# Where and when the raw words of w_val and w_out are loaded, and when w_val's are converted

## The chip, the cores and the metric

The kernel runs on one core of a Trainium2 chip. The metric is the device time in microseconds (us) of one execution. Five engines work beside each other, each through its own list of instructions in order: PE (TensorE, matrix multiplications), ACT (ScalarE), DVE (VectorE), POOL (GpSimd), and SP (SyncE), which here issues every transfer (DMA). An instruction waits at the head of its engine's list until what it needs is there, and everything behind it waits too.

## The reference

Three stages are applied to four batches of 576 positions and 512 features (8 heads of 64), all float32 at the interface.

- Attention: a low-resolution attention over positions averaged by four, repeated four times, plus a local attention in which position i sees positions i-3 to i+3.
- A Fourier mixing and an MLP: `u = x + real(fft over positions and features)`, `un` = `u` normalized over features, then `u + relu(un @ w_ch1) @ w_ch2` (512 to 2048 to 512).
- A gated projection: `gate = sigmoid(5-tap causal convolution over positions)`, output `(gate * (x @ w_val)) @ w_out` (both 512 x 512).

The weights come in as 64-bit floats; the kernel gets them as pairs of 32-bit words, low word and high word, and has to make float32 of them itself.

## The kernel before, in words

The MLP is cut into 12 units of 192 positions, three per batch. A unit's first product (`ph`, line 1047, in groups of 24 matmuls) and second product (`pc`, line 1065) are each made of three 16-bit products, because every float32 operand is split into a 16-bit high part and a 16-bit rest (`hh` and `hl`, `uh` and `ul`, `yh` and `yl`; of weights `hi` and `lo`). Each group of `pc` therefore needs `hh`, which ACT writes (line 1051), and `hl`, which DVE writes (line 165, called from `h_group`). The first unit alone is computed in float32 (`steps32`, lines 1009 and 1022), while the weights are still being split.

The weights pass through four steps: a transfer brings raw words, 1024 words of 64 bits per row and position for w_ch1 and w_ch2, 2 x 512 for w_val and w_out; three DVE instructions make float32 of a raw tile (`to_f32`: a TENSOR_SCALAR at line 283, then two SCALAR_TENSOR_TENSORs at line 165); a norm of the whole matrix gives a power of two; and `conv_w` writes `hi` (ACT, line 344) and `lo` (DVE, line 165). There are 20 positions: 0 to 7 hold w_ch1, 8 to 15 w_ch2, 16 and 17 w_val, 18 and 19 w_out. Their storage is W0 and a ring of ten double tiles; the tile named W17 in the lists below holds `W[17]` and `W[18]`, the one named W19 holds `W[19]` and `W[20]`. `hi` and `lo` of position i go into the storage `W[i]`, while the float32 values of that position sit in `W[i+1]`. So the split of one position must be finished by DVE before ACT can start the next: the 16 splits of w_ch1 and w_ch2 are one chain that goes back and forth between ACT and DVE.

While the first unit runs, batch 1's attention runs beside it. Its local attention goes in three groups: band and scores on PE (`dS`), maximum on DVE (`dmx`), exponentials on ACT (line 536), normalization on DVE (`dP`, line 168), transposes on PE (`dPT`), a copy on ACT (`PT`, line 563), products with v on PE (`dO`), copies into X on ACT (line 583). The squares of v for the pooled v are ACT's at line 425; its sums are POOL's. After each unit the five convolution taps of the gated stage follow: products on ACT (`tap`, line 1123), sums on POOL (line 171).

In the kernel before, the raw words of w_val and w_out land in the two tiles of the tag "k" and "v" in the pool `qkv`, which hold batch 1's windows of v until the local attention's last products have read them. `word_w` issues each load and its conversion together, half a position at a time, so eight loads and 24 DVE instructions. The order of the program is made by a list of events, each with a place in units of the MLP: `spread` lays a list of steps evenly over a stretch. The table's entry `S_W3 = (1.02, 1.6)` lays all steps of `weights3_steps` over the second unit. A scheduler then sets each engine's list from this order, from priorities (`urgent`) and from its own estimate of time.

Of the kernel before, what the change touches and what calls it, by code (L numbers as in the profile page):

```python
# [12 lines left out]
I32 = mybir.dt.int32  # L13
# [4 lines left out]
B, H, S, D = 4, 8, 576, 64  # L18
# [31 lines left out]
S_S0 = (-11.1, -10.1)  # L50
# [3 lines left out]
S_END = -8.95  # L54
S_F0 = (-8.9, -8.1)
# [1 line left out]
S_N0 = -7.5  # L57
S_W2 = (-7.4, -6.9)
S_C2 = (0.89, 0.94)
S_W3 = (1.02, 1.6)  # L60
N_WARM = (8, 5, 14, 2, 2, 2)
S_G1 = (-6.8, -6.7)
S_G2 = (0.2, 0.44)
# [12 lines left out]
P_TAP = (-0.05, 0.35)  # L76
# [51 lines left out]
def attn_moe_kernel(ctx, tc, q_t, k_t, v_t, w1, w2, w_val, conv_t, w_out, c_feat, c_seq, c_band, c_eye, out):  # L128
    nc = tc.nc
    P = 128  # L130
    w1, w2, w_val, conv_t, w_out = (x.bitcast(I32) for x in (w1, w2, w_val, conv_t, w_out))

    def pool(name, bufs=1, **kw):
        return ctx.enter_context(tc.tile_pool(name=name, bufs=bufs, **kw))
# [29 lines left out]
    def stt(eng, out, in0, scalar, in1, op0, op1):  # L164
        return eng.scalar_tensor_tensor(out=out, in0=in0, scalar=scalar, in1=in1, op0=op0, op1=op1)  # L165
# [16 lines left out]
    def load(**kw):  # L182

        if chain["on"] and chain["last"] is not None:
            with tc.issue_after(chain["last"]):
                i = nc.sync.dma_start(**kw)
        else:
            i = nc.sync.dma_start(**kw)
        chain["last"] = i.ins
# [63 lines left out]
    NPOS = 20  # L253
    ring = [wp.tile([P, 2048], F32, name=f"W{2 * i + 1}") for i in range(NPOS // 2)]
    W = [wp.tile([P, 1024], F32, name="W0")]
# [11 lines left out]
    def rows(dst, src, c, c0, n):  # L267
        load(out=dst, in_=src[c * 128:(c + 1) * 128, 2 * c0:2 * (c0 + n)])
# [3 lines left out]
    def behind(gate, f):  # L272

        if gate is None:
            f()
        else:
            with tc.issue_after(gate):
                f()

    def to_f32(dst, raw, gate=lambda: None):  # L280

        r = raw.rearrange("p (n t) -> p n t", t=2)
        behind(gate(), lambda: V.tensor_scalar(out=dst, in0=r[:, :, 1], scalar1=3, scalar2=0x3FFFFFF8,  # L283
                                               op0=ALU.logical_shift_left, op1=ALU.bitwise_and))
        behind(gate(), lambda: stt(V, dst, r[:, :, 1], -0x40000000, dst, ALU.bitwise_and, ALU.bitwise_or))
        behind(gate(), lambda: stt(V, dst, r[:, :, 0], 29, dst, ALU.logical_shift_right, ALU.bitwise_or))
# [18 lines left out]
    def word_w(i):  # L305
        if i < 16:
            raw = raws.pop(i)
            n = 1024 // len(raw)
            for z, x in enumerate(raw):
                to_f32(W[i + 1].bitcast(I32)[:, z * n:(z + 1) * n], x,  # L310
                       lambda g=(gates, gates2)[i // 8]: g.pop(0) if len(g) > 1 else g[0])
            return
        assert "scored" in st[1]
        for a in range(2):
            raw = qkv.tile([P, 1024], I32, tag="kv"[a], name="raw")
            rows(raw, w_val if i < 18 else w_out, (i % 2) * 2 + a, 0, 512)
            to_f32(W[i + 1].bitcast(I32)[:, a * 512:(a + 1) * 512], raw)

    gram = {}

    def sumsq_w(i, key, first, last):

        if first:
            gram[key] = pst("cv", [P, P]) if key == "wo" else ps_c.tile([P, P], F32, tag="c1", name="gram")
        x = W[i + 1].bitcast(BF16).rearrange("p (n t) -> p n t", t=2)
        for c in range(8):
            blk = x[:, c * 128:(c + 1) * 128, 1]
            behind(st[0]["st2"].ins if i < 8 else None, lambda: T.matmul(
                out=gram[key], lhsT=blk, rhs=blk, start=(first and c == 0), stop=(last and c == 7)))
# [11 lines left out]
    def conv_w(i, s, eng):  # L341

        h_, l_, r_ = hi(i), lo(i), W[i + 1]
        A.activation(out=h_, in_=r_, func=AF.Copy, scale=s[:, 0:1])
        if eng is G:
            A.activation(out=r_, in_=r_, func=AF.Copy, scale=s[:, 0:1])
            G.tensor_tensor(out=l_, in0=r_, in1=h_, op=ALU.subtract)
        else:
            stt(eng, l_, r_, s[:, 0:1], h_, ALU.mult, ALU.subtract)
# [17 lines left out]
    def wv_scale():  # L367
        ps = pst("cv", [P, 512])
        for a in range(4):
            j = pr_t("sqv", [P, 512])  # L370
            A.activation(out=j, in_=W[17 + a // 2][:, (a % 2) * 512:(a % 2) * 512 + 512], func=AF.Square)
            T.matmul(out=ps, lhsT=ones, rhs=j, start=(a == 0), stop=(a == 3))
        mx = keep.tile([P, 1], F32, name="cvmx")
        V.tensor_reduce(out=mx, in_=ps, axis=AX.X, op=ALU.max)
        mx2 = keep.tile([P, 1], F32, name="cvmx2")
        V.tensor_scalar(out=mx2, in0=mx, scalar1=float(DM), scalar2=None, op0=ALU.mult)
        sc["sv"], sc["ivv"] = pow2(mx2, 14, "wv")

    def wo_scale():
        f = trace_w("wo")  # L380
        sc["so"], sc["ivo"] = pow2(f, 14, "wo")
        ivvo = keep.tile([P, 1], F32, name="ivvo")
        mul(V, ivvo, sc["ivv"], sc["ivo"])
        sc["ivvo"] = ivvo
# [3 lines left out]
    st = {}  # L388
# [524 lines left out]
    un = {}  # L913
    mainp = {}

    def main_pools():
        for n, bufs in (("un", 2), ("hg", 3), ("g", 1), ("L", 2), ("tap", 3), ("S", 3)):
            mainp[n] = pool("m_" + n, bufs)

    def l_t(name, shape):  # L920
# [289 lines left out]
    def w_in2(i):  # L1210
        if i >= 11:
            load_w(i)
        word_w(i)

    def w_in(i):
        word_w(i)
# [4 lines left out]
    def weights3_steps():  # L1221
        def first():
            to_f32(cw.rearrange("p a b -> p (a b)").bitcast(I32), craw)

        def a2():
            wv_scale()
            for i in range(16, 18):
                conv_w(i, sc["sv"], G if i in LO_G else V)

        def a3():  # L1230
            for i in range(18, NPOS):
                sumsq_w(i, "wo", i == 18, i == NPOS - 1)
            wo_scale()
            for i in range(18, NPOS):
                conv_w(i, sc["so"], G if i in LO_G else V)
        return [first] + [lambda i=i: word_w(i) for i in range(16, NPOS)] + [a2, a3]

    units = [(b, j) for b in range(B) for j in range(UPB)]
    events = []
# [1 line left out]
    def put(pos, f):  # L1241
        events.append((pos, len(events), f))

    def spread(steps, p0, p1):
        tot = sum(c for c, _ in steps)
        acc = 0.0
        for c, f in steps:
            put(p0 + (p1 - p0) * acc / tot, f)
            acc += c
# [16 lines left out]
    def close():  # L1266
        start.close()
        main_pools()

    assert S_LD[1] <= S_T0[0] and S_L1 <= S_W1[0] and S_T0[1] <= S_S0[0] and S_S0[1] <= S_F0[0] and S_F0[1] <= S_N0  # L1270
    assert S_W1[1] <= S_W2[0] and 8 / 17 < S_C1[0] and S_C1[1] <= S_C2[0] and 15 / 17 < S_C2[0]
    assert S_S0[1] <= S_END <= S_F0[0] and S_C2[1] <= min(S_W3[0], 1 + P_TAP[0])
    put(S_END, close)
    for b in range(1, B):
        steps = attn_steps(b)
# [7 lines left out]
        spread(steps[n1:], *P_E[b])  # L1283
        put(P_L[b], lambda b=b: urgent(lambda: ln(b, 0), "N"))
    w3 = weights3_steps()
    spread([(1.0, f) for f in w3], *S_W3)
    for n, (b, j) in enumerate(units):
        main = mlp_steps(b, j)
        spread([(1.0, f) for f in main], n, n + 1)
# [63 lines left out]
```

## Time and profile before

| | us |
|---|---|
| median of 3 runs | 771.54 (769.82 to 771.86) |
| the profiled execution, its own time | 768.35 |
| its span in the trace | 766.5 |
| PE busy | 695.8 |
| DVE busy | 450.3 |
| ACT busy | 378.1 |
| POOL busy | 183.8 |

Times in the trace count from the start of the span. The first 110 us go to batch 0's attention and Fourier stage, the first unit runs from about 109 to 178 us with batch 1's local attention, and units of 16-bit products follow. Matmuls are pipelined, so a busy share of PE near 100% does not say that it runs at its peak; an idle PE from 110 us on lengthens the kernel unless it makes the time up later.

### The profile page before, as it was taken

Reading aid. Unit: us, or ns where it says so; the run is one execution under the profiler, and the core shown is the slowest. Engines: PE = TensorE matmul, PEld = TensorE weight load, DVE = VectorE, ACT = ScalarE, POOL = GpSimd, SP = SyncE. Lnnn points to the kernel's source line nnn. Section 1 sums busy time; section 2 is a strip of 40 time slices with the busy share of each in tenths; the row PEclk is TensorE's granted clock in tenths of the full one; section 3 lists DMA queues with packets and bytes.
Section 4 is the critical chain, followed back from the end, with each engine's and each line's share of the span. In section 5 each row is a group of like instructions: output and inputs, shape, how many; then the busy total and the mean of one; then the engine's idle time right before and its main releaser. Section 6 shows DMA issues by size and latency. Waiting matters only on the chain.

```text
span 766.5 us, 18498 instructions
## 1 busy us (share of the span) xinstructions
PE 695.8 (91%) x7811; PEld 605.4 (79%) x7811; DVE 450.3 (59%) x897; ACT 378.1 (49%) x1170; POOL 183.8 (24%) x187
## 2 busy tenths in 40 slices
PE   6869579986699998999979999898999999999996
PEld 3535459985688987987869899788799998999893
DVE  3894789769885766256786631656742472532134
ACT  1465211778544636677552766864522435251512
POOL 0400000015421522361231243601410323030300
PEclk8565579999799999999999999999899999999999
DMA  9965347033321110222121001001100000000001
GB/s 227 370 226 166 112 185 208 24 101 117 102 74 56 55 64 16 54 93 77 39 69 64 16 23 34 22 2 54 55 15 2 16 1 30 2 15 2 29 1 42
DMA packets 29004, 54.79 MB, mean 71 GB/s; under 512 B 2133, under 2 KB 17109, under 8 KB 27898
## 3 DMA queue, kind: packets, MB, share of 16 engines
q1 hardware_dynamic: 28922, 53.61, 21.6%
q8 instruction: 61, 1.00, 0.5%
q14 instruction: 21, 0.17, 0.1%
HBM read 46.52 MB, written 9.45 MB: 73 GB/s over the span
## 4 chain that ended last, share of the span: by engine, by line
PE 61%; DVE 20%; ACT 8%; DMA 7%; issue 1%; SPq 1%; POOL 0%; ACTq 0%; DVEq 0%; POOLq 0%
PE pc L1065 19%; PE ph L1047 18%; DVE W L165 6%; PE val L1144 5%; PE out L1160 5%; ACT dP L536 3%; PE po L716 2%; DMA v<-in_v_dram 2%; DVE W L283 2%; DVE fF L787 1%; ACT tap L1123 1%; PE dO L577 1%; PE sc L668 1%; DMA raw<-in_moe_w_out_dram 1%; PE ab L810 1%
## 5 line engine op out<-in xcount | busy, mean ns | idle before, releaser
L1065 PE MATMUL pc<-hh,W 128*128 128x192 f16 x1408 | 199.4, 248 | 3.8 <-ACT hh L1051 3.8
L1065 PEld LDWEIGHTS <-W 128*128 128x128 f16 x2112 | 178.0, 99 | 25.6 <-issue 21.8
L1047 PE MATMUL ph<-uh,W 128*128 128x192 f16 x1408 | 196.4, 247 | 0.1
L1065 PE MATMUL pc<-hl,W 128*128 128x192 f16 x704 | 173.3, 249 | 12.7 <-DVE hl L165 12.7
L1047 PEld LDWEIGHTS <-W 128*128 128x128 f16 x2112 | 176.4, 98 | 7.1 <-issue 5.1
L1047 PE MATMUL ph<-ul,W 128*128 128x192 f16 x704 | 173.7, 247 | 0.0
L171 POOL TENSOR_TENSOR W<-W,tap 128x768 f32<-128x768 f32 x40 | 74.9, 1873 | 141.2 <-ACT tap L1123 109.8
L165 DVE SCALAR_TENSOR_TENSOR hl<-ph,hh 128x384 f16<-128x384 f32 x88 | 48.0, 551 | 98.4 <-ACT hh L1051 98.2
L1051 ACT ACTIVATE hh<-ph 128x384 f16<-128x384 f32 x88 | 42.3, 485 | 72.0 <-PE ph L1047 71.6
L1123 ACT ACTIVATE tap<-X,cw 128x192 f32<-128x192 f32 x180 | 66.5, 446 | 5.5 <-DMA out_dram<-osb 4.7
L1144 PE MATMUL val<-yy,W 128*128 128x192 f16 x576 | 53.3, 246 | 4.0 <-ACT yy L1099 2.3
L1144 PEld LDWEIGHTS <-W 128*128 128x128 f16 x576 | 48.0, 98 | 5.1 <-issue 3.9
L536 ACT ACTIVATE dP<-dS,dmx 128x64 f32<-128x64 f32 x160 | 47.7, 332 | 0.3
L1160 PE MATMUL out<-W,gh 128*128 128x512 f16 x144 | 45.9, 379 | 0.0
L536 ACT ACTIVATION_READ_ACCUMULATOR dP<-dS,dmx 128x1 f32 x160 | 36.2, 226 | 0.0
L1160 PE MATMUL out<-W,gl 128*128 128x512 f16 x72 | 27.3, 379 | 2.1 <-DVE gl L165 2.1
L165 DVE SCALAR_TENSOR_TENSOR W<-W,W 128x1024 int32<-128x1024 int32 x24 | 28.7, 1215 | 0.1
L171 POOL TENSOR_TENSOR vr<-v 72x256 f32<-72x256 f32 x12 | 11.3, 944 | 66.9 <-DMA v<-in_v_dram 64.2
L165 DVE SCALAR_TENSOR_TENSOR yy<-X,s_y,yy 128x768 f16<-128x768 f32 x12 | 19.2, 1601 | 13.5 <-ACT yy L1099 13.4
L682 ACT ACTIVATE E<-sc,nm 72x144 f32<-72x144 f32 x64 | 23.5, 372 | 4.8 <-PE po L716 4.7
L716 PE MATMUL po<-ET,vr 72*64 72x144 f32 x128 | 21.6, 345 | 4.6 <-ACT ET L711 4.6
L1009 PE MATMUL ph<-u,W 128*128 128x192 f32 x128 | 24.8, 350 | 1.0 <-DVE u L945 1.0
(222 smaller groups left out, 1212.4 us busy)
## 6 DMA issues: line engine op xcount, KB each, us to landing
W<-in_moe_w_ch_dram SPq DMA_DIRECT2D x12, 1024.0 KB
v<-in_v_dram SPq DMA_DIRECT2D x32, 144.0 KB
out_dram<-osb SPq DMA_DIRECT2D x18, 256.0 KB
vw<-in_v_dram SPq DMA_DIRECT2D x16, 256.0 KB
X<-in_q_dram SPq DMA_DIRECT2D x6, 576.0 KB
kT<-in_k_dram SPq DMA_DIRECT2D x4, 582.0 KB
dx<-X SPq DMA_DIRECT2D x4, 576.0 KB
dr<-dx SPq DMA_DIRECT2D x4, 576.0 KB
```

The costliest lines, as they stand in the source:

```text
L165: return eng.scalar_tensor_tensor(out=out, in0=in0, scalar=scalar, in1=in1, op0=op0, op1=op1)
L171: return eng.tensor_tensor(out=out, in0=a, in1=b, op=ALU.add)
L536: A.activation(out=s_[:, z, a], in_=pss[par][:, z, a], func=AF.Exp, scale=SCALE, bias=mx[:, par, z, a:a + 1], accum_out=su[:, par, z, a:a ...
L682: A.activation(out=E[:, qc], in_=ps[:, qc], func=AF.Exp, scale=SCALE / 16, bias=nm[:, qc:qc + 1], accum_out=su[:, qc:qc + 1],)
L716: T.matmul(out=po[par * 64:par * 64 + 64], lhsT=d["vr"][:, kc, (a % 2) * 4 + (a // 2) * 2 + par], rhs=ets[par][:, kc], start=(kc == 0), st ...
L1009: i = T.matmul(out=ps[:, e], lhsT=W[kc * 2 + m // 8 + 1][:, o:o + 128], rhs=u()[:, kc, :], start=(kc == 0), stop=(kc == 3))
L1047: T.matmul(out=ps[:, e], lhsT=w1_ap(pw, kc, 2 * g + e), rhs=uh[px][:, kc, :], start=(t == 0), stop=(t == 11))
L1051: A.activation(out=h_, in_=ps, func=AF.Relu)
L1065: T.matmul(out=ps[m // 2][:, m % 2], lhsT=w2_ap(pw, kk, m), rhs=x[px][:, e, :], start=(kk == 0 and (pw, px) == (0, 0) and m % 2 == 0), sto ...
L1123: A.activation(out=g[:, c], in_=X[:, c, c0:c0 + UT], func=AF.Copy, scale=cw[:, c, t:t + 1])
L1144: T.matmul(out=ps[:, e], lhsT=wv_ap(pw, kc, 2 * mh + e), rhs=m_["y"][px][:, kc, :], start=(t == 0), stop=(t == 11))
L1160: T.matmul(out=ps, lhsT=(gh, gl)[px][:, kc, t * 128:(t + 1) * 128], rhs=wo_ap(pw, kc), start=(n == 0), stop=(n == 11))
```

## The change

The step that loads is cut off from the step that converts. `load_w3(i, a)` picks where half a of position i lands: halves (16, 0) and (17, 1) in `W[19]`, halves (16, 1) and (18, 0) in `W[20]`, both free since w_ch2's last raw words were converted; halves (17, 0) and (18, 1) in a new tile `rx`; only the two halves of position 19 still in the tiles "k" and "v". The steps come in two lists with places of their own: w_val's loads and conversions lie over 0.44 to 0.8, within the first unit, and w_out's, with the norms and splits of both, over 1.0 to 1.5.

```diff
-S_W3 = (1.02, 1.6)
+S_W3 = ((0.44, 0.8), (1.0, 1.5))
...
-        assert "scored" in st[1]
         for a in range(2):
+            to_f32(W[i + 1].bitcast(I32)[:, a * 512:(a + 1) * 512], raw3.pop((i, a)))
+
+    raw3 = {}
+
+    def load_w3(i, a):
+
+        if (i, a) in ((16, 0), (17, 1)):
+            raw = W[19].bitcast(I32)
+        elif (i, a) in ((16, 1), (18, 0)):
+            raw = W[20].bitcast(I32)
+        elif i < 19:
+            raw = mainp["rx"].tile([P, 1024], I32, tag="rx", name="raw")
+        else:
+            assert "scored" in st[1]
             raw = qkv.tile([P, 1024], I32, tag="kv"[a], name="raw")
-            rows(raw, w_val if i < 18 else w_out, (i % 2) * 2 + a, 0, 512)
-            to_f32(W[i + 1].bitcast(I32)[:, a * 512:(a + 1) * 512], raw)
+        raw3[i, a] = raw
+        rows(raw, w_val if i < 18 else w_out, (i % 2) * 2 + a, 0, 512)
...
-        for n, bufs in (("un", 2), ("hg", 3), ("g", 1), ("L", 2), ("tap", 3), ("S", 3)):
+        for n, bufs in (("un", 2), ("hg", 3), ("g", 1), ("L", 2), ("tap", 3), ("S", 3), ("rx", 1)):
...
-        return [first] + [lambda i=i: word_w(i) for i in range(16, NPOS)] + [a2, a3]
+        ld = lambda *h: lambda: [load_w3(*x) for x in h]
+        return ([ld((16, 0), (16, 1), (17, 0)), first, lambda: word_w(16), ld((17, 1)), lambda: word_w(17)],
+                [ld((18, 0), (18, 1), (19, 0), (19, 1)), a2, lambda: word_w(18), lambda: word_w(19), a3])
...
-    spread([(1.0, f) for f in w3], *S_W3)
+    for g, p in zip(w3, S_W3):
+        spread([(1.0, f) for f in g], *p)
```

The list of DVE shows two places where instructions moved. The first is in the first unit, from the last step of w_ch1's power of two (`s_w1` precedes it) to the normalization of batch 1's first group of local attention (`dP1`). Before:

```order
L168 TENSOR_TENSOR uc_1269<-uc_1269,r0_1285 128x768
L539 TENSOR_SCALAR dsu_1241<-dsu_1241 128x8
L540 RECIPROCAL dsu_1241<-dsu_1241 128x8
L168 TENSOR_TENSOR dP1_1245<-dP1_1245,dsu_1241 128x256
L168 TENSOR_TENSOR dP1_1250<-dP1_1250,dsu_1241 128x256
L165 SCALAR_TENSOR_TENSOR W0_122<-W1_112,s_w1_1182,W0_122 128x1024
L974 TENSOR_TENSOR ul_1297<-uc_1269,uh_1296 128x768
```

Now (raw_1553 is the new tile `rx`; W17 from W19 converts a half that lies in the ring):

```order
L168 TENSOR_TENSOR uc_1272<-uc_1272,r0_1288 128x768
L552 TENSOR_SCALAR dsu_1244<-dsu_1244 128x8
L165 SCALAR_TENSOR_TENSOR W17_120<-W19_121,W17_120 128x512
L283 TENSOR_SCALAR W17_120<-raw_1553 128x512
L165 SCALAR_TENSOR_TENSOR W0_122<-W1_112,s_w1_1185,W0_122 128x1024
L553 RECIPROCAL dsu_1244<-dsu_1244 128x8
L165 SCALAR_TENSOR_TENSOR W17_120<-W19_121,W17_120 128x512
L987 TENSOR_TENSOR ul_1300<-uc_1272,uh_1299 128x768
L165 SCALAR_TENSOR_TENSOR W17_120<-raw_1553,W17_120 128x512
L283 TENSOR_SCALAR W17_120<-W19_121 128x512
L168 TENSOR_TENSOR dP1_1248<-dP1_1248,dsu_1244 128x256
L168 TENSOR_TENSOR dP1_1253<-dP1_1253,dsu_1244 128x256
```

With those that stand ahead of the first row shown, four line-283 instructions and five of line 165 on half a position, the split of position 0 and `ul` now come before the first normalization; the first of them (line 283 on half (16, 0)) stands where the power of two's shift by `p2d` ended. On PE, six of the last eight float32 `ph` matmuls now stand ahead of the transposes `dPT` that read this normalization. The rest of position 17 and half (18, 0) are converted right behind, then half (18, 1) ahead of the second group's normalization.

The second place is the end of the first unit, up to the first `hl` of the second. Before:

```order
L283 TENSOR_SCALAR W17_120<-raw_2225 128x512
L165 SCALAR_TENSOR_TENSOR W11_117<-W13_118,s_w2_1528,W11_117 128x1024
L165 SCALAR_TENSOR_TENSOR W17_120<-raw_2225,W17_120 128x512 x2
L283 TENSOR_SCALAR W17_120<-raw_2095 128x512
L165 SCALAR_TENSOR_TENSOR W17_120<-raw_2095,W17_120 128x512 x2
L945 TENSOR_TENSOR uc_1819<-X_129,st_1822 128x768
L283 TENSOR_SCALAR W19_121<-raw_2259 128x512
L165 SCALAR_TENSOR_TENSOR W13_118<-W13_118,s_w2_1528 128x1024
L165 SCALAR_TENSOR_TENSOR hl_1940<-ph_1913,hh_1938 128x384
```

Now:

```order
L165 SCALAR_TENSOR_TENSOR W11_117<-W11_117,s_w2_1531 128x1024
L283 TENSOR_SCALAR W19_121<-raw_1941 128x512
L165 SCALAR_TENSOR_TENSOR W19_121<-raw_1941,W19_121 128x512 x2
L958 TENSOR_TENSOR uc_1842<-X_129,st_1845 128x768
L165 SCALAR_TENSOR_TENSOR W11_117<-W13_118,s_w2_1531,W11_117 128x1024
L165 SCALAR_TENSOR_TENSOR hl_1970<-ph_1943,hh_1968 128x384
L165 SCALAR_TENSOR_TENSOR hl_2045<-ph_2018,hh_2043 128x384
```

Before, raw_2095 is a half of w_val in a tile of batch 1's v; now raw_1941 is half (19, 1) of w_out in the same tile. Between the end of the first unit and the first `hl` one conversion now stands in full where two and a line-283 instruction stood, and the splits there are of positions 11 and 12 where they were of 12 and 13.

## Rows read from the trace of the kernel before

**Rows 1.** Page, busy us (share of the span) and instructions of each engine

```profile
PE 695.8 (91%) x7811; PEld 605.4 (79%) x7811; DVE 450.3 (59%) x897; ACT 378.1 (49%) x1170; POOL 183.8 (24%) x187
```

**Rows 2.** Windows: stretch, length, busy us of each engine, PE clock, DMA share, GB/s

```profile
180.00:200.00 20.00, 7.23 (x66) 6.50 (x66) 19.44 (x19) 16.70 (x47) 13.93 (x10) 0.71 0.33 109
...
400.00:500.00 100.00, 96.30 (x1281) 85.73 (x1279) 52.73 (x97) 61.36 (x215) 38.12 (x42) 1.00 0.09 31
```

**Rows 3.** Waits from 178 to 240: who waited for whom, us, times, longest

```profile
PE pc L1065 <- DVE hl L165: 9.3, 1, 9.3
...
PE pc L1065 <- ACT hh L1051: 1.9, 1, 1.9
```

**Rows 4.** Chain of waits from 178 to 198: start, us, what

```profile
178.88 1.15 PE dO L577 x64
...
180.05 4.70 DMA raw<-in_moe_w_val_dram
...
184.77 2.87 DVE W L283
...
187.67 2.19 DVE W L165
...
189.88 1.10 DVE W L165
190.97 0.86 DVE uc L945
191.84 2.45 DVE W L283
194.29 2.74 DVE W L165
197.03 0.47 DVE hl L165
```

**Rows 5.** Timeline of POOL: start, us, instruction, count, idle before

```profile
185.55 3.75 POOL L171 TENSOR_TENSOR tap<-tap 128x768 f32<-128x768 f32 x2
...
192.20 3.75 POOL L171 TENSOR_TENSOR tap<-tap 128x768 f32<-128x768 f32 x2
```

**Rows 6.** Timeline of DVE within the first unit

```profile
133.54 1.21 DVE L165 SCALAR_TENSOR_TENSOR W<-W,W 128x1024 int32<-128x1024 int32 x1
...
137.62 0.14 DVE L235 TENSOR_SCALAR p2d<-p2c 128x1 int32<-128x1 int32 x1
...
139.83 0.76 DVE L168 TENSOR_TENSOR dP<-dP,dsu 128x256 f32<-128x256 f32 x2
...
143.01 1.28 DVE L165 SCALAR_TENSOR_TENSOR W<-W,s_w 128x1024 f16<-128x1024 f32 x1 [0.35 <-ACT W L344]
...
151.43 0.17 DVE L539 TENSOR_SCALAR dsu<-dsu 128x16 f32<-128x16 f32 x1 [4.04 <-ACT dP L536]
```

**Rows 7.** Timeline of PE within the first unit

```profile
143.77 0.60 PE L557 MATMUL dPT<-eye,dP 128*128 128x128 f32 x4
144.21 2.77 PE L1009 MATMUL ph<-u,W 128*128 128x192 f32 x16
...
168.00 1.92 PE L577 MATMUL dO<-PT,vw 64*64 64x58 f32 x48 [1.33 <-ACT PT L563]
...
175.20 2.77 PE L1022 MATMUL pc<-h,W 128*128 128x192 f32 x16
```

**Rows 8.** Timeline of ACT, end of the first unit

```profile
167.25 0.69 ACT L563 ACTIVATE PT<-dPT 128x512 f32<-128x512 f32 x1
...
179.90 4.26 ACT L1123 ACTIVATE tap<-X,cw 128x192 f32<-128x192 f32 x12
...
187.38 0.47 ACT L1051 ACTIVATE hh<-ph 128x384 f16<-128x384 f32 x1
```

**Rows 9.** Conversions from raw, 168 to 222: duration ns min/median/max, first and last start

```profile
L165 DVE SCALAR_TENSOR_TENSOR W<-raw,W x16: 668/678/2176, 175.8 to 220.8; 128x512 int32<-128x512 int32 x16
L283 DVE TENSOR_SCALAR W<-raw x8: 410/423/2862, 175.4 to 217.4; 128x512 int32<-128x512 int32 x8
```

More of the change, by code (lines that the diff above doesn't have):

```diff
@@ L1271, in attn_moe_kernel @@
     assert S_W1[1] <= S_W2[0] and 8 / 17 < S_C1[0] and S_C1[1] <= S_C2[0] and 15 / 17 < S_C2[0]
-    assert S_S0[1] <= S_END <= S_F0[0] and S_C2[1] <= min(S_W3[0], 1 + P_TAP[0])
+    assert S_S0[1] <= S_END <= S_F0[0] and S_C2[1] <= min(S_W3[1][0], 1 + P_TAP[0])
     put(S_END, close)
```

## The prediction

> **What bounds the kernel now.** I read the page's busy shares first, then the windows, the waits around the thinnest window, and the chain through it. PE is busy 91% of the span and no other engine over 59% [rows 1]: from the first unit on, PE's list sets the end, and a change of the weights' preparation is worth what PE waits for it. Later stretches have little to give (96.3 of 100 us busy between 400 and 500), but from 180 to 200 PE works only 7.23 us of 20, at a mean clock of 0.71 [rows 2], so between its two levels of 1.2 and 2.4 GHz. The largest wait there is PE's for the first `hl` of the second unit, 9.3 us, after 1.9 us for `hh` [rows 3]. The chain says what made `hl` late. PE's last `dO` of batch 1 ends at 180.03 and frees a tile of v; only then can a half of w_val be loaded into it, 4.70 us; then DVE does, in its list's order, this conversion, `uc`, another line-283 instruction and a split, and `hl` last, ending at 197.50: 17.5 us from `dO` to `hl` [rows 4]. None but `hl` is what PE waits for.
>
> These instructions are slow there: 2.87 us for a line-283 instruction whose median is 0.42, and 2.19 for a line-165 one whose median is 0.68 [rows 4, 9]. POOL's sums of taps run beside them, two from 185.55 and two from 192.20, 1.87 us each [rows 5]; the first line-283 instruction ends at 187.6, when POOL's first sum is over, the second at 194.3, when its third is.
>
> **The change, part by part.** The sum is made against the profiled execution, 768.35 us with a span of 766.5, which lies 3.2 below the median of 771.54; the difference is then carried to the median. No work is added: eight loads and 24 conversions stay, in other places. So every term is a shift of PE.
>
> *The loads in the ring.* Half (16, 0) can be loaded when w_ch2's last raw words in that tile are converted: DVE starts that at 133.54 and ends at 134.75 [rows 6]. SP has nothing else to wait for there. At 4.70 us a load [rows 4] it lands at 139.4. DVE comes to its conversion at 137.7, behind `p2d` [rows 6]. So DVE waits 1.7 us at the head of its list; behind it stand w_ch1's power of two, the splits and the first group's normalization. The bounds: nothing, if the load takes 3.0 us or less, and 3 us, if transfers of v still fill the queues. I take 1.7.
>
> *The conversions in the first unit.* Ahead of the first normalization come four line-283 and five line-165 instructions, 4 x 0.42 + 5 x 0.68 = 5.1 us, less about 0.08 each because neighbours overlap (the rows of one pass start closer than they last): 4.4. The split of position 0 and `ul`, which came after the normalization, now come before it: from its end at 140.5 to the idle 0.35 before 143.01, 2.15 us [rows 6]. The normalization started at 139.83 and now would at 139.83 + 1.7 + 4.4 + 2.15 = 148.1. PE reached its transposes at 143.77; now six of eight `ph` matmuls come first, 6/8 of 2.77 = 2.1 us [rows 7], so 145.9. PE waits some 2.4 us there, where it did not wait before.
>
> The lateness travels on. The second group's maximum stands behind the normalization on DVE, so its exponentials on ACT start about 4 us later. DVE's idle 4.04 us before 151.43 [rows 6] covers that, but half (18, 1) is converted in front of the second normalization, and it can only be loaded when `rx` has been read, near 151.8: it lands at 156.5 and DVE waits again. From there the splits alternate between ACT and DVE at about 2.5 us each with nothing to spare, and two or three of them precede the third group's maximum. I put the third group's `PT`, 167.25 before, at 172 to 173, 5 us later. PE already waited 1.33 us for it and started its `dO` at 168.00 [rows 7, 8]. After that `dO` the new list of PE has 15 float32 `pc` matmuls left where it had 19, 4 x 0.35 = 1.4 us less (0.35 from 2.77 for 8, a float32 matmul being two records). So the first unit ends 5 - 1.4 = 3.6 us later: 177.97 [rows 7] becomes 181.6. Bounds: 0 and +5.
>
> *The queue before the first `hl`.* One line-283 instruction of 2.45 us goes [rows 4]. The rest of the chain stays, with w_out in w_val's place: half (19, 1) lands in the same tile of v, freed by the same `dO`. With `dO` ending at 184.7, it lands at 189.4. Two prices follow. Free of POOL: 0.42 + 2 x 0.60 + 0.86 + a split of 1.28 + 0.47 gives `hl` at 193.7, but ACT now holds it. Its list has the 12 taps before `hh`; they took 4.26 us from 179.90, and `hh` came 7.5 us after their start [rows 8]. The taps wait for X, whose update on DVE stands behind the split of position 10; I put them at 185.3, so `hh` at 193 to 193.5 and `hl` at 194.8 with the split between. All beside POOL, at the chain's prices: 2.87 + 2.19 + 1.10 + 0.86 + 2.74 + 0.47 = 10.2, `hl` at 199.7. I take 196.7, two of POOL's sums in the way, against 197.50: PE gains 0.8, with bounds of 2.7 gained and 2.2 lost. The clock's loss after the wait stays, since the wait shrinks and does not go.
>
> What each price rests on is named by the Trainium skill, SBUF — State Buffer (SBUF: two separate sides): DVE and GpSimd share one port pair as an exclusive lock, and a DVE instruction in a two-port mode or with two SBUF inputs is blocked for the whole of a GpSimd one that reads SBUF. The trace agrees: the two line-283 instructions end as POOL's sums end, while `hl`, with one input in PSUM, kept its 0.47. By this rule alone, every conversion that meets a sum pays its remainder, which is the second rival below.
>
> *The second unit.* Four halves of w_val, 12 instructions and some 6.5 us of DVE, leave the stretch around and behind the wait, so `hl` of later groups has fewer in front. PE had little idle time left there; I take 0.5 gained, between 0 and 1. Against it, `val` of unit 0 now needs a `yl` that stands on DVE behind the end of the second unit: between 0 and 1.5 lost, I take 0.3. The order behind that shifts by one to three microseconds of PE's work until 600 us; its sign I can't tell, 0 with 3 either way.
>
> *Sum*: -0.8 - 0.5 + 0.3 = -1.0. 768.35 becomes 767.3, and the median 771.54 becomes 770.5. The likeliest case's own range is 767.5 to 773.5.
>
> The skill also has a price for a load that would soften the first term: DMA: Bandwidth & Descriptors (Anatomy of one DMA) gives about 2 us fixed and 436 GB/s for another issuing path, by estimate 3.2 us for these 512 KB. The load would land at 138.0 and DVE would wait 0.3. The measured 4.70 decides here.
>
> **The rivals.**
> - *The first unit swallows it* (faster). For it: DVE is idle 4.04 us at one place [rows 6], PE has float32 work to go on with. If the unit ends at 178 as before, the shortened queue stands whole: from its end to `hl` 196.7 - 181.6 = 15.1 instead of 19.5, so -4.4, and -0.2 for the rest: 766.9. If also no POOL sum is in the way, another 2: 765. Against it: DVE and ACT are strict lists and the first new instruction waits for a load.
> - *The wait changes its cargo* (slower). w_out's half, loaded after the same `dO`, meets POOL's sums at full price: +2.2 from `hl` at 199.7. PE's new waits in the first unit pull the rest along, `val` pays its 1.5, and w_out's late halves delay nothing else: +3.7, 775.2. It decides itself by whether the half lands before POOL's first sum of taps starts. Against it: the sums also start later, since X is later.
> - *Nothing moves but the place of the wait*: within 0.3%, with PE's idle time merely divided between first unit and second, 771 to 773. For it: total work is unchanged, and ACT's taps alone hold `hh` back.
>
> **How the numbers follow.** A measurement here tells from no change what exceeds 0.3%, 2.3 us, so 769.2 and 773.9 are the bounds. Forecast 0.38, of which 0.12 falls below 769.2; first unit swallows it 0.29; changed cargo 0.25; only moved 0.08. Faster: 0.12 + 0.29 = 0.41. Slower: 0.25. Same: 0.34. The range takes in most of both outer cases and the 3 us of the later order: 763.5 to 776.5.
>
> **What would show it.** Right: in the changed profile PE waits 2 to 3 us for a `dP` near 146, the first unit's last `pc` ends near 181, the chain before the first `hl` leads back over a transfer from w_out to a `dO`, and PE's wait for `hl` is 5 to 8 us instead of 9.3. Wrong: if PE does not wait for `dP`, the first rival holds; if the wait before the first `pc` is under 4 us, I priced the queue too high; if it is 10 or more, the second rival holds. If PE's idle time between 260 and 600 changes by over 3 us, the order behind the second unit decided and not these terms.

## The result, and the profile after

The changed kernel takes 779.37 us (777.63 to 779.90, 4 runs) against 770.68 us (768.59 to 771.86, 4 runs) of the kernel before: a ratio of 1.0112, 95% interval 1.0083 to 1.0141. It is slower by 8.7 us where I had forecast 1 us faster. Its interval lies clear of 1. The profiled execution spans 777.0 us, 10.5 more than the one before.

The first row is the page's busy time after, which answers to [rows 1]; the two below it are windows of the changed kernel (stretch, length, busy us of PE, PEld, DVE, ACT and POOL, PE clock, DMA share, GB/s), the first of which answers to [rows 2].

```profile
PE 698.9 (90%) x7811; PEld 607.0 (78%) x7811; DVE 455.9 (59%) x897; ACT 379.5 (49%) x1170; POOL 183.8 (24%) x187
...
180.00:200.00 20.00, 8.58 (x96) 7.49 (x87) 15.61 (x20) 16.65 (x44) 8.35 (x9) 0.74 0.45 117
245.00:272.00 27.00, 23.39 (x270) 22.15 (x268) 25.13 (x30) 16.24 (x38) 14.08 (x11) 0.94 0.22 67
```

The second window of the kernel before:

```profile
245.00:272.00 27.00, 27.00 (x348) 26.63 (x346) 19.80 (x42) 18.24 (x41) 10.89 (x12) 1.00 0.26 74
```

The stretch that I priced, 180 to 200, looks better: PE works 8.58 us there instead of 7.23. But PE also comes to the first unit 1.84 us earlier (first `ph` at 107.30 instead of 109.14), ahead of every instruction that moved. The loss stands where PE had been full: at 245 to 272, where batch 1's input for the Fourier mixing is made. (DVE and POOL write `fs` and DVE `fF`, sums and differences of X; ACT and DVE split `fF` into the 16-bit parts `FH` and `FL`; PE's `ab` reads these.) To see how much is lost where, take three matmuls that both kernels have: the first `pc` with `hl`, and two `st` (line 939, now 952) with which a norm begins. The kernel before, then the changed one (start, us, instruction, idle before and what ended it):

```profile
197.55 0.32 PE L1065 MATMUL pc<-hl,W 128*128 128x192 f16 x1 [9.33 <-DVE hl L165]
...
285.58 0.59 PE L939 MATMUL st<-uc,ones 128*128 128x192 f32 x2 [0.22 <-DVE uc L171]
...
475.82 0.59 PE L939 MATMUL st<-uc,ones 128*128 128x192 f32 x2 [0.38 <-ACT X L583]
```

```profile
196.39 0.32 PE L1078 MATMUL pc<-hl,W 128*128 128x192 f16 x1 [4.93 <-DVE hl L165]
...
290.97 0.59 PE L952 MATMUL st<-uc,ones 128*128 128x192 f32 x2 [0.30 <-DVE uc L171]
...
485.81 0.59 PE L952 MATMUL st<-uc,ones 128*128 128x192 f32 x2 [0.38 <-ACT X L596]
```

At the first `hl` the changed kernel is 1.2 us ahead, less than the 1.84 with which it came to the first unit. From there to the first `st` it takes 94.6 us instead of 88.0, and from that to the second 194.8 instead of 190.2; behind it the two run alike (291.2 and 290.7 to the end). I call these stretches A and B: +6.6 and +4.6.

An `st` can stand elsewhere in another list, so A and B don't hold the same work. Of the 3347 matmuls of both stretches, 965 lie in A before and 945 in the changed kernel. PE, when full, does 348 in 27.00 us (the last window above), 0.078 us each; by this estimate 1.6 us of work went from A to B, and with equal work the losses are 8.1 and 3.1. The changed kernel and e13 below, whose lists are equal, differ by 1.2 in A, so smaller differences mean nothing.

**Stretch A.** The second unit's taps go through the storage `W[20]` (in `conv`, `g = W[NPOS]` for all units but the first and the last). The float32 values of position 19 of w_out lie there until its last split has read them. Before, ACT and POOL:

```profile
260.00 1.49 ACT L1123 ACTIVATE W<-X,cw 128x192 f32<-128x192 f32 x4 [0.39 <-DVE W L165]
```

```profile
261.57 5.59 POOL L171 TENSOR_TENSOR W<-W,tap 128x768 f32<-128x768 f32 x3 [7.74 <-ACT W L1123]
```

The tap waits for that split, and POOL's sums start at 261.57, when all but the tail of DVE's `fs`, `fF` and `FL` is over. Now, with w_out prepared at 1.0 to 1.5, the split ends 11 us sooner. ACT, POOL and DVE of the changed kernel:

```profile
249.04 1.49 ACT L1136 ACTIVATE W<-X,cw 128x192 f32<-128x192 f32 x4 [0.74 <-DVE W L165]
```

```profile
250.61 1.94 POOL L171 TENSOR_TENSOR W<-W,tap 128x768 f32<-128x768 f32 x1 [3.62 <-ACT W L1136]
...
256.80 2.13 POOL L171 TENSOR_TENSOR W<-W,tap 128x768 f32<-128x768 f32 x1
...
261.58 4.41 POOL L171 TENSOR_TENSOR W<-W,tap 128x768 f32<-128x768 f32 x2
```

```profile
248.93 0.75 DVE L792 TENSOR_TENSOR fs<-X 128x577 f32<-128x577 f32 x1
...
250.81 2.36 DVE L792 TENSOR_TENSOR fs<-X 128x577 f32<-128x577 f32 x1
...
254.02 0.82 DVE L800 TENSOR_TENSOR fF<-fs 128x289 f32<-128x289 f32 x2
254.76 0.81 DVE L165 SCALAR_TENSOR_TENSOR FL<-fF,s_x,FH 128x578 f16<-128x578 f32 x1
...
257.18 2.44 DVE L800 TENSOR_TENSOR fF<-fs 128x289 f32<-128x289 f32 x2
...
261.96 2.37 DVE L165 SCALAR_TENSOR_TENSOR FL<-fF,s_x,FH 128x578 f16<-128x578 f32 x1
264.25 2.43 DVE L800 TENSOR_TENSOR fF<-fs 128x289 f32<-128x289 f32 x2
```

An `fs`, a pair of `fF` and an `FL` take 0.75 to 0.82 us alone and 2.36 to 2.44 each where they meet a sum. PE waits for `FL` and `FH` (2.01, 0.30 and 1.28 us), and when it goes on its clock is low. PE's first of these waits, and the window behind it:

```profile
260.41 0.46 PE L823 MATMUL ab<-feat,FL 128*97 128x129 f16 x2 [2.01 <-DVE FL L165]
```

```profile
260.00:264.00 4.00, 3.59 (x24) 3.28 (x24) 4.00 (x3) 2.19 (x6) 3.92 (x3) 0.57 0.25 51
```

In 245 to 272 PE is idle 27.00 - 23.39 = 3.6 us, and 0.06 of 27 us, 1.6, go with the clock: 5.2 us of A's loss. The rest of it is not traced.

### The profile page after: what moved, and what is told of

Same layout as the page of the kernel before. It is cut to its first block, busy times and chain, and to the rows that moved or that the text cites. A ratio compares the mean times of both kernels' runs of the same rounds, so it can differ in the third digit from the quotient of the medians.

```text
span 777.0 us, 18493 instructions
## 1 busy us (share of the span) xinstructions
PE 698.9 (90%) x7811; PEld 607.0 (78%) x7811; DVE 455.9 (59%) x897; ACT 379.5 (49%) x1170; POOL 183.8 (24%) x187
## 4 chain that ended last, share of the span: by engine, by line
PE 54%; DVE 21%; DMA 15%; ACT 6%; issue 2%; POOL 2%; SPq 1%; POOLq 0%; ACTq 0%
PE pc L1078 19%; PE ph L1060 16%; DVE W L165 7%; PE out L1173 5%; PE val L1157 4%; DMA W<-in_moe_w_ch_dram 3%; DMA dr<-dx 3%; DMA v<-in_v_dram 2%; DMA dx<-X 2%; ACT dP L549 2%; PE sc L681 1%; DVE W L283 1%; PE po L729 1%; DVE fF L800 1%; DMA raw<-in_moe_w_ch_dram 1%
## 5 line engine op out<-in xcount | busy, mean ns | idle before, releaser
L1078 PE MATMUL pc<-hh,W 128*128 128x192 f16 x1408 | 202.7, 251 | 4.1 <-ACT hh L1064 4.1
L1078 PE MATMUL pc<-hl,W 128*128 128x192 f16 x704 | 175.2, 251 | 12.5 <-DVE hl L165 12.5
L165 DVE SCALAR_TENSOR_TENSOR W<-W,W 128x1024 int32<-128x1024 int32 (+1 forms) x30 | 32.8, 1109 | 0.1
L171 POOL TENSOR_TENSOR vr<-v 72x256 f32<-72x256 f32 x12 | 9.6, 803 | 77.7 <-DMA v<-in_v_dram 76.9
L165 DVE SCALAR_TENSOR_TENSOR yy<-X,s_y,yy 128x768 f16<-128x768 f32 x12 | 19.6, 1636 | 13.9 <-ACT yy L1112 13.8
L681 PE MATMUL sc<-qkT 64*72 64x144 f32 x128 | 24.7, 334 | 1.6 <-DVE qkT L601 1.0
L1164 ACT ACTIVATE gh<-W 128x384 f16<-128x384 f32 x20 | 10.6, 528 | 31.2 <-DVE W L165 31.2
```

The lines of the kernel that those rows point to most:

```text
L171: return eng.tensor_tensor(out=out, in0=a, in1=b, op=ALU.add)
L681: T.matmul(out=pss[par][:, qc], lhsT=d["qkT"][r, 0, a, qc * QC:(qc + 1) * QC], rhs=d["qkT"][r, 1, a, :], start=True, stop=True,)
L1078: T.matmul(out=ps[m // 2][:, m % 2], lhsT=w2_ap(pw, kk, m), rhs=x[px][:, e, :], start=(kk == 0 and (pw, px) == (0, 0) and m % 2 == 0), sto ...
L1164: A.activation(out=gh, in_=g, func=AF.Copy, scale=2.0 ** -16)
```

## The experiments

A and B are the two stretches, in us; before has 88.0 and 190.2, the changed kernel 94.6 and 194.8. Then come the matmuls that lie in A, and A and B with 965 of them there (an estimate, 0.078 us for each that is moved; the changed kernel: 96.1 and 193.3). Ratios are to the kernel before.

| run | us | ratio (95%) | A | B | matmuls in A | A, equal work | B, equal work |
|---|---|---|---|---|---|---|---|
| e1_taps_late | 766.51 | 0.9964 (0.9945 to 0.9983) | 88.0 | 190.6 | 933 | 90.4 | 188.1 |
| e2_small_sums | 769.11 | 0.9982 (0.9958 to 1.0006) | 87.8 | 192.2 | 956 | 88.5 | 191.5 |
| e3_wout_late | 772.85 | 1.0040 (1.0021 to 1.0059) | 89.5 | 194.1 | 927 | 92.4 | 191.1 |
| e4_old_time | 768.56 | 1.0000 (0.9975 to 1.0025) | 87.4 | 191.2 | 965 | 87.4 | 191.2 |
| e5_taps_vals_late | 776.57 | 1.0086 (1.0059 to 1.0112) | 86.4 | 200.1 | 933 | 88.8 | 197.6 |
| e6_second_late | 772.49 | 1.0047 (1.0029 to 1.0066) | 89.8 | 194.5 | 934 | 92.2 | 192.0 |
| e7_free_taps | 778.46 | 1.0118 (1.0097 to 1.0139) | 91.3 | 196.9 | 983 | 89.9 | 198.3 |
| e8_sums_dve | 772.98 | 1.0058 (1.0035 to 1.0081) | 91.6 | 192.5 | 976 | 90.7 | 193.3 |
| e9_old_early | 774.09 | 1.0062 (1.0039 to 1.0084) | 85.6 | 196.4 | 936 | 87.9 | 194.2 |
| e10_before_free_taps | 774.35 | 1.0067 (1.0043 to 1.0091) | 90.1 | 192.0 | 954 | 90.9 | 191.1 |
| e11_hair | 777.95 | 1.0115 (1.0075 to 1.0155) | 95.8 | 192.8 | 982 | 94.5 | 194.1 |
| e12_later_yet | 768.52 | 0.9981 (0.9966 to 0.9997) | 86.9 | 191.4 | 965 | 86.9 | 191.4 |
| e13_small_3 | 777.23 | 1.0094 (1.0065 to 1.0123) | 93.4 | 193.5 | 945 | 95.0 | 192.0 |
| e14_small_1_3 | 768.12 | 0.9973 (0.9949 to 0.9998) | 87.7 | 191.1 | 956 | 88.4 | 190.4 |
| e15_before_small_3 | 768.25 | 0.9980 (0.9952 to 1.0008) | 87.9 | 189.8 | 965 | 87.9 | 189.8 |

**e1, e2: take the sums away from the Fourier input.**

```diff
             ps = list(P_T0)
+        if n == 1:
+            ps[0] = (0.2, 0.55)
```

> The changed kernel, with the second unit's five convolution taps put at 0.2 to 0.55 behind the unit instead of -0.05 to 0.35, so that POOL's four sums of taps stand behind batch 1's Fourier input and not in it. Theory A (what was lost lies at 247 to 268 us, where the sums, set free early because W[20] is read for the last time at 249 us instead of 260, hold DVE's fs, fF and FL at 1.8 to 2.4 us each): fs, fF and FL are back at 0.75 to 0.8, PE's three waits for FL and FH (3.6 us) and the drop of its clock to 0.57 at 260 to 264 are gone, and the time is 771 to 774. Rival B (the loss is spread over later units, and this place is only where it first shows): 777 to 780. Rival C (the new waits in the first unit cost it): 778 to 780, and the waits for FL and FH stay.

```diff
-                add(G, m_["g"], m_["g"], g)
+                w = 16 if i == 1 else UT
+                add(G, m_["g"][:, :, 0:w], m_["g"][:, :, 0:w], g[:, :, 0:w])
```

> The changed kernel, but POOL's sums of taps of the second unit add only 16 of 192 positions (the other sums of that unit are left out); they stay at their places in POOL's list. Theory A (these sums beside DVE's Fourier input cost about 7 us): DVE's fs, fF and FL at 250 to 266 last 0.75 to 0.8 us each instead of up to 2.44, PE does not wait for FL, time 771 to 774. Rival B (DVE is late there because of what its list holds, not because of POOL): the instructions get faster but PE still waits over 2 us for FL, 776 to 779. Rival C (first unit): 778 to 780.

Both gave more than expected: the whole loss of time went. With equal work e2 keeps 0.5 us of A's 8.1 and 1.3 of B's 3.1. In e1 the second unit's gated product stands partly ahead of its last sums and so uses an unfinished gate. In e2 every engine's order is the changed kernel's up to the first of these sums, and the sums are short; behind it POOL's second sum stands ahead of its first `fs`, and one `FL` ahead of an `fF`. DVE and POOL of e2, and its window:

```profile
250.15 0.87 DVE L792 TENSOR_TENSOR fs<-X 128x577 f32<-128x577 f32 x1
...
258.40 0.94 DVE L800 TENSOR_TENSOR fF<-fs 128x289 f32<-128x289 f32 x2
```

```profile
249.96 0.45 POOL L171 TENSOR_TENSOR W<-W,tap 128x64 f32<-128x64 f32 x1 [3.62 <-ACT W L1136]
```

```profile
245.00:272.00 27.00, 27.00 (x345) 26.59 (x343) 20.07 (x34) 16.40 (x39) 6.90 (x13) 1.00 0.33 106
```

W[20] is free as early as in the changed kernel, and PE is full. The early start alone costs nothing; the length of the sums does (with the small changes of order that came with it, which no run separates).

**e3, e4, e6, e12: put the lists elsewhere.** `S_W3` is ((0.44, 0.8), (1.02, 1.7)) in e3, ((1.02, 1.25), (1.25, 1.6)) in e4, ((0.44, 0.8), (1.25, 1.6)) in e6 and ((1.02, 1.3), (1.3, 1.7)) in e12; the places of the raw words are the changed kernel's.

> The changed kernel with the second list (w_out's loads and conversions, norms and splits of both) at 1.02 to 1.7 instead of 1.0 to 1.5; w_val's stays in the first unit. The last split, which frees W[20] for the taps, then comes later, and POOL's list has both fs ahead of the sums of taps. Theory A: no sum of taps beside fs, fF and FL of batch 1, 771 to 775 us. Rival C (the conversions in the first unit cost the time, wherever w_out's stand): 778 to 780. Rival B (every new order loses some): 776 to 780.

> The changed kernel's places of the raw words (ring halves, the new tile, two halves in k and v), but at the old time: the first list at 1.02 to 1.25 and the second at 1.25 to 1.6. POOL's list has both fs ahead of the sums of taps, as in the kernel before. Theory A: no collision at batch 1's Fourier input; the first unit has no new wait for a dP; only the queue before the first hl differs, so 768 to 772. Rival D (the storage itself costs, by loads that come at other times): 776 to 780. Rival B (every new order loses some): 774 to 780.

> The changed kernel with the second list at 1.25 to 1.6; the first list stays at 0.44 to 0.8. Against e4_old_time this gives w_val's place in the first unit alone, against the changed kernel the place of the second list alone. Theory A: the last split of w_out is at 258 to 262 us again, the sums of taps follow behind FL, 767 to 771. Rival C (w_val's conversions in the first unit cost time): 773 to 778, with more waiting in the first unit than e4 has.

> The changed kernel's storage with the lists at 1.02 to 1.3 and 1.3 to 1.7, so w_out still later than in e4_old_time (768.6). Theory A: no sum ahead of FL, nothing waits for w_out before val and out need it, 766 to 770. Rival: the first gated products wait for w_out, 771 to 775.

e4 and e12 are level with the kernel before, so the new storage costs nothing. But e12 is no later place: its lists are e4's, instruction for instruction (DVE, ACT, POOL, SP, and PE from the first unit on), so it is e4 once more, and what differs between the two is what executions differ by. I had expected no wait for a `dP` in e4. It is there, since the scheduler put w_val's conversions into the first unit although the table has them behind it. DVE and PE of e4:

```profile
138.83 0.43 DVE L283 TENSOR_SCALAR W<-W 128x512 int32<-128x512 int32 x1 [0.27 <-DMA W<-in_moe_w_val_dram]
```

```profile
146.69 0.44 PE L570 MATMUL dPT<-eye,dP 128*128 128x128 f32 x2 [3.23 <-DVE dP L168]
```

So e4 has the conversions in the first unit and PE's wait for them, and loses nothing by it: what separates it from the changed kernel is chiefly when w_out is ready. e3 and e6 have their sums behind `FL` too, yet a ratio of 1.004 and 1.005, and with equal work an A of 92.4 and 92.2, so half of A's loss can come about without any sum: there an `hl` stands behind w_out's first split and the `fF` on DVE, and PE waits 2.0 and 2.6 us for it at 256. The expectation of 767 to 771 for e6 was missed, and its time lies just below the 773 from which I'd have put it down to w_val's conversions; e4 has these too and loses nothing.

**e7, e10: bring the sums in without the early split.** In both the second unit's taps get a tile of their own instead of W[20], e7 on the basis of e4, e10 on the kernel before.

```diff
-                if i in (0, B * UPB - 1):
+                if i in (0, 1, B * UPB - 1):
```

> e4_old_time (second list at 1.25 to 1.6, 768.6 us) with one edit: the second unit's taps use a tile of their own pool and not W[20], so they need not wait for w_out's last split. POOL's list has one sum between the two fs and three right behind. Theory A: the sums run beside fF and FL though w_out is prepared late; those instructions take up to 2.4 us, PE waits 1 to 4 us for FL or FH, 771 to 776. Rival F (the early preparation of w_out itself, by DVE's load, made the loss, and the sums are a bystander): 767 to 770, no wait for FL.

> The kernel before with one edit: the second unit's taps use a tile of their own pool instead of W[20], so that nothing of w_out holds them. POOL's list has the four sums right behind its second fs, so they start some 5 us earlier than before and run beside the last two fF and FL. Theory A: those last 1.5 to 2.4 us each, PE waits 1 to 3 us for FL between 255 and 270, 771 to 775. Rival F (bystander): no wait there, 768 to 770. Rival B: the difference comes behind 280 us.

e10 is the counterpart of e2; its lists are those of the kernel before up to the first sum. Its DVE, POOL and window:

```profile
259.11 2.37 DVE L165 SCALAR_TENSOR_TENSOR FL<-fF,s_x,FH 128x578 f16<-128x578 f32 x1
...
263.60 2.37 DVE L165 SCALAR_TENSOR_TENSOR FL<-fF,s_x,FH 128x578 f16<-128x578 f32 x1
265.88 0.54 DVE L165 SCALAR_TENSOR_TENSOR hl<-ph,hh 128x384 f16<-128x384 f32 x1
```

```profile
258.46 2.40 POOL L171 TENSOR_TENSOR tap<-tap 128x768 f32<-128x768 f32 x1 [2.96 <-ACT tap L1123]
262.53 6.99 POOL L171 TENSOR_TENSOR tap<-tap 128x768 f32<-128x768 f32 x3 [1.67 <-ACT tap L1123]
```

```profile
245.00:272.00 27.00, 24.27 (x313) 23.81 (x311) 23.49 (x41) 18.22 (x38) 12.86 (x10) 1.00 0.22 63
```

With w_out prepared as late as ever, two `FL` meet sums, PE idles 2.7 us where it was full, and the time lies in the 771 to 775 that I expected. So the sums' meeting with the Fourier input costs by itself, without w_out's early end. How much is less clear than the 0.67% suggest: of the 5.5 us by which e10's trace is longer, 1.9 stand ahead of the first `hl`, where the lists are the same, 2 in A (2.9 with equal work) and 1.8 in B. e7 has the meeting too (A is 3.9 above e4, 2.5 with equal work), but loses more in B, 5.7 (7.1); its 778.46 lies above the 771 to 776 that I expected.

**e5, e8: candidates for a repair.** e5 is e1 with the product moved behind the sums (`ps[:2] = (0.2, 0.55), (0.56, 0.8)`); e8 gives the second unit's sums to DVE (`add(V if i == 1 else G, ...)`).

> The changed kernel with the second unit's taps at 0.2 to 0.55 and its gated product at 0.56 to 0.8, so that the product stands behind all sums again (in e1_taps_late its first half stood ahead of the last ones). Nothing else. Theory A (POOL's sums beside batch 1's Fourier input are the whole loss): no sum between 245 and 262 us, PE waits under 0.5 us for FL and FH, and the time is that of e1, 765 to 769. Rival E (e1 was quick because the product did not wait for its sums): 771 to 775.

> The changed kernel with the second unit's four sums of taps on DVE instead of POOL. Theory A (what hurts is two engines on one port, 1.9 us a sum): a sum takes DVE 0.75 to 0.95 us, four of them 3.0 to 3.8 us of its list instead of the 8 us that fs, fF, FL and gl lost; PE's waits for FL and FH shrink from 3.6 to 0 to 2 us, 768 to 773. Rival G (DVE is simply too full at this place, whoever holds it up): 776 to 780.

e5 missed both of its ranges. With equal work it repairs A (88.8, level with the kernel before within noise) and loses 7.4 us in B, where PE waits 7.07 us at once for an `FL` of batch 2. So e1's 766.51 can't be taken for a repair: with the gate finished ahead of the product, the same move of the sums gives 776.57. That the moved work holds up this `FL` is not shown. e8 is at the upper end of its 768 to 773. It recovers 3 us of A (5.4 with equal work): on DVE the sums take 0.94 to 2.17 us each, 5.8 together, where I had put 3.0 to 3.8.

**e9, e11, e13 to e15: what stretch B hangs on.** e9 is the kernel before with its list at (1.02, 1.5); e11 the changed kernel with (1.0, 1.52) for (1.0, 1.5). e13 and e14 are e2's edit for `i == 3` and for `i in (1, 3)`, e15 the former in the kernel before.

> The kernel before with its one list at 1.02 to 1.5 instead of 1.02 to 1.6: w_out is prepared earlier, but the raw words still land in k and v. POOL's list keeps both fs ahead of the second unit's sums. Theory A (what costs is sums beside the Fourier input): no sum ahead of FL, 768 to 772. Rival F (an early end of w_out's preparation costs by itself): 774 to 779. Rival B (the lists fall otherwise and each new one loses something later): 772 to 778, lost behind 280 us.

> The changed kernel with the second list at 1.0 to 1.52 instead of 1.0 to 1.5: next to no change of purpose, but POOL's list now has two sums ahead of the first fs, one between and one behind. Theory A: the sums still run beside the Fourier input, so PE is behind by 4 to 8 us at 262 us; what it loses behind 280 us shows how much of the changed kernel's second loss (4 to 5 us between 300 and 420) belongs to its lists: 771 to 781, and if that second loss follows from the first, 777 to 781. If it belongs to the one list, 771 to 776.

> The changed kernel, but POOL's four sums of taps of the fourth unit (beside batch 2's Fourier input, 390 to 405 us) add only 16 of 192 positions; the rest of them is left out. The lists up to there stay. Same cause (the second loss is these sums too): PE's waits between 390 and 410 shrink from 6 to 2 us or less, its clock does not fall at 400, 773 to 776, and the gain is 2 us or more above that of e15. Another cause (the second loss lies in many small waits from 320 on that the lists bring): the gain is the same as e15's, so 777 to 779 if that is 1 to 2.

> The changed kernel with the sums of the second and of the fourth unit cut to 16 of 192 positions (the rest left out). Theory A: e2's 769 less e15's gain, 764 to 768. Rival B: 769 to 773, as the lists fall otherwise again.

> The kernel before with the fourth unit's sums cut to 16 of 192 positions (the rest left out), as the measure for e13. There the sums at 389 to 393 hold up the norm's r and with it FL (PE waits 2.6 us). If the sums cost as much here as there: 2 to 4 us gained, 765 to 768. If they cost nothing that PE would not wait for otherwise: 768 to 770.

e9 has no sum beside batch 1's Fourier input and an A like that of the kernel before, with equal work. It missed the 768 to 772 of theory A: it loses 6 us in B (4.0 with equal work), with this wait of PE in batch 2's Fourier input, where the kernel before waits 2.6:

```profile
396.46 0.34 PE L810 MATMUL ab<-feat,FL 128*97 128x128 f16 x1 [6.96 <-DVE FL L165]
```

So B can be lost without A. Whether the changed kernel's part follows from A's is not settled: e11 has the collision again and with equal work 6.5 us lost in A and 3.9 in B, and its 777.95 lies in the range that I had given for a B that follows. The fourth unit's sums are not it: e13's lists are the changed kernel's throughout, and it gains 0.2% over it, as much as e15 over the kernel before, well inside both intervals. e14, at 768.12 between its two ranges, adds nothing clear of noise to e2's 769.11. In e13 the wait only changes its name. PE's longest wait between 380 and 410 in the changed kernel and in e13:

```profile
PE pc L1078 <- DVE hl L165: 3.1, 1, 3.1
```

```profile
PE val L1158 <- ACT yy L1112: 2.7, 1, 2.7
```

Stretch B before and in the changed kernel, and the 4 us behind that wait of 3.1 us:

```profile
285.58:475.82 190.24, 180.57 (x2382) 158.52 (x2382) 108.98 (x213) 115.97 (x409) 62.92 (x66) 1.00 0.15 47
```

```profile
290.97:485.81 194.84, 184.29 (x2402) 161.50 (x2402) 108.79 (x214) 116.24 (x409) 63.05 (x66) 0.99 0.16 46
...
399.70:403.70 4.00, 4.00 (x34) 3.90 (x34) 0.64 (x1) 1.74 (x5) 0.10 (x1) 0.59 0.35 135
```

Of B's 4.6 us only 0.9 are more idle time of PE (10.55 instead of 9.67). The other 3.7 are busy time: 1.6 by estimate the 20 matmuls more, and 0.41 of 4.00 us, 1.6, the clock behind that wait. B ranges over 190 to 200 us in these kernels (188 to 198 with equal work), with the lists that the scheduler makes after any edit. Why the changed kernel's list has this wait of 3.1 us is left open.

## Why the prediction was wrong, step by step

*The step that failed* is "the order behind that shifts by one to three microseconds of PE's work until 600 us; its sign I can't tell, 0 with 3 either way". It shifted by 11.2: 6.6 in A and 4.6 in B, with equal work 8.1 and 3.1. B's part is about what the step allowed. A's is more, and it is no chance of the order. It follows from the change and could be read ahead: in the trace of before ACT's tap at 260.00 waits for the DVE split of w_out, and POOL's sums wait for the tap. I asked what w_val's departure takes off DVE (a credit of 0.5 us for a lighter second unit), and never what w_out's earlier end sets free. My last sentence on what would show it wrong, PE's idle time between 260 and 600, pointed near the place, but by its letter it stayed silent: that time rose by 2.9 us (16.0 to 18.9), under its 3, as much of the loss is slow clock or stands ahead of 260. e1 and e2 show the cause of A's part, and e10 that the sums cost without w_out's early end; B's part is told in its waits and clock, and its cause stays open. The price of a sum beside a DVE instruction stood in my own text, for another place.

*The loads in the ring.* DVE does wait at the head of its list, but the agreement in size is luck: I had one wait of 1.7 us for one load of 4.70, and there are two, 0.78 and 1.03 us for two loads, 1.8 together. The first load, issued at 132.91, lets DVE go on at 136.25, 3.3 us later; the second, issued at 133.30, took 5.77. DVE's first two conversions and the normalization, and PE's wait for it:

```profile
136.25 0.43 DVE L283 TENSOR_SCALAR W<-W 128x512 int32<-128x512 int32 x1 [0.78 <-DMA W<-in_moe_w_val_dram]
...
139.09 0.43 DVE L283 TENSOR_SCALAR W<-W 128x512 int32<-128x512 int32 x1 [1.03 <-DMA W<-in_moe_w_val_dram]
...
145.59 1.28 DVE L168 TENSOR_TENSOR dP<-dP,dsu 128x256 f32<-128x256 f32 x2
```

```profile
146.59 0.44 PE L570 MATMUL dPT<-eye,dP 128*128 128x128 f32 x2 [2.64 <-DVE dP L168]
...
175.35 1.47 PE L1035 MATMUL pc<-h,W 128*128 128x192 f32 x8
```

*The conversions in the first unit.* PE waits 2.64 us for `dP`, against 2.4: right. The lateness did not travel as far as I had it: the load into `rx` made DVE wait no second time, and the third group's `dO` started without a wait. The unit lasts 0.7 us longer (107.30 to 176.82 against 109.14 to 177.97) and not 3.6. Its price was too high.

*The queue before the first `hl`.* Right in the chain, wrong in size; that `hl` is read at 196.39, forecast 196.7, is luck. PE came to the first unit 1.84 us early, and from the unit's last `pc` to the first `hl` it takes 19.6 us (176.82 to 196.39), as before (177.97 to 197.55), where I had 15.1. Nothing was gained. The chain leads back over a transfer from w_out, and ACT's X holds PE first, 4.8 us instead of 1.6. The waits from 178 to 240 that answer to [rows 3], then the chain that answers to [rows 4]:

```profile
PE pc L1078 <- DVE hl L165: 4.9, 1, 4.9
...
PE st L952 <- ACT X L596: 4.8, 1, 4.8
...
PE pc L1078 <- ACT hh L1064: 1.7, 1, 1.7
```

```profile
182.25 4.99 DMA raw<-in_moe_w_out_dram
...
187.26 2.53 DVE W L283
...
189.81 2.87 DVE W L165
...
192.70 1.10 DVE W L165
193.81 0.88 DVE uc L958
```

The wait for `hl` is just under my 5 to 8 us, since the wait for X stands in front of it. The load is issued only at 182.25, 1.9 us behind the last `dO` (180.36), since SP has loads of v in front of it that wait for ACT, and it takes 4.99. From 187.26 to the first `hl` it is 9.1 us where I had 7.3 from the landing: two of POOL's sums are in the way, as I had taken, and the conversions pay them 2.53 and 2.87 instead of 0.42 and 0.68. One reading in that part of the prediction was wrong: `hl`'s 0.47 bore out nothing, since POOL's last sum there ended at 192.20 + 3.75 = 195.95 and `hl` started at 197.03. e10 bears it out: `hl` takes 0.54 at 265.88, within three sums on POOL.

*The rivals.* "The wait changes its cargo" had the sign, and for the queue the mechanism: w_out's half meets the sums at full price. It had not the place of the loss; its 775.2 would have been reached by other terms. "The first unit swallows it" was right on the unit, 0.7 us longer, and wrong on the shorter queue that it built on. That the first `hl` comes 1.2 us earlier is within what executions differ by: e10, with the same lists up to there, has it 1.9 us later than the kernel before.

## What to carry to other kernels

When a step is moved, list the tiles that it sets free as well as those that it needs, and find in the trace of before who waits for them: a wait that nobody pays for may be what keeps two engines apart. What is released early should be followed to the next place where it can meet a critical chain. And where a scheduler makes the lists, expect every edit to cost or give some microseconds elsewhere; compare matmuls that both kernels have, stretch by stretch, and count the work between them, before a difference in the total is put down to the edit.

## What the runs showed of the hardware

The rule of the Trainium skill that the prediction cites (SBUF — State Buffer, section "SBUF: two separate sides") holds at this place too: a sum on POOL makes an `fs` or `FL` of 0.8 us last up to 2.4, and the `fs` from 250.81 ends 0.62 us behind the sum from 250.61, nearly its own length. `hl`, which reads PSUM, takes 0.54 within e10's three sums. POOL pays as well: its sums take 1.81 us alone and 1.94 to 2.40 beside these instructions of DVE. Of the ten rows of `fs`, `fF` and `FL` in the changed kernel four meet a sum, and the stretch costs PE 3.6 us of waiting and 1.6 of clock.

The clock I had not expected: one wait of 2.01 us was followed by 4 us at a mean granted clock of 0.57, nearer the lower of the two levels, and one of 3.1 us by 4 us at 0.59. In e10 two waits of 1.35 and 1.38 us left the 27 us at 1.00, and in the kernel before a wait of 2.6 us at 394.6 left 394 to 402 at 1.00, so the length of the wait alone does not tell.
